# Queries of later groups loaded in 2-KB packets and put in order by four copies, and stores of two batches moved behind the loads

## The chip, the cores and the metric

The kernel runs on one core of one Trainium2 chip. The metric is device time in microseconds; the median of several executions is compared. One execution is also profiled, and its trace gives the instructions of each engine: TensorE (PE, with its weight loads as PEld), VectorE (DVE), ScalarE (ACT), GpSimd (POOL), and SyncE (SP), which here only issues DMAs.

## The reference

A decaying linear attention over 4 batches, 8 heads, 768 positions and 64 elements a head, followed by a mixture-of-depths feed-forward on its output, seen as 4 x 768 rows of 512.

```python
for b in range(nb):                       # blocks of 64 positions
    intra = einsum('bhic,bhjc->bhij', qb, kb) * Dmask[None]
    intra = einsum('bhij,bhjd->bhid', intra, vb)
    inter = einsum('bhid,bhde->bhie', qb * lam_pow[None], kv_state)
    out[:, :, sl] = intra + inter
    kv_state = lam_block * kv_state + einsum('bhsd,bhse->bhde', kb * rev_pow, vb)
...
scores = einsum('bsd,d->bs', x, w_gate)   # x: the attention's output, (4, 768, 512)
for b in range(B):
    top_idx = argpartition(-scores[b], capacity)[:capacity]   # capacity 128
    xe = x[b, top_idx]
    ye = maximum(xe @ w1, 0.0) @ w2       # 512 -> 1024 -> 512
    out[b, top_idx] = xe + sigmoid(scores[b, top_idx])[:, None] * ye
```

Everything is float32.

## The kernel before

**Groups.** The work is cut into 24 groups (NG) of 128 positions with all eight heads, six (NT) to a batch; group g belongs to batch g // 6. Groups 0 to 10 are "wide" (one state step for 128 positions), groups 11 to 23 work in two halves of 64 positions (WIDE = 11). The Python loop at L682 writes the order of every engine's instructions by hand (a manual schedule); nothing is reordered later, and each engine works through its own list and waits on semaphores.

**Loads.** `load(g)` (L66) issues three DMAs of 256 KB from SP: keys (kn), queries (qn), values (vn). Each tile has the 128 positions as partitions and the 8 x 64 elements of the heads behind each other, so that the DRAM side is 1024 runs of 64 floats (256 bytes). Eight sets of tiles exist (AHEAD), and `loads_to` (L656) decides how many groups ahead the loads stand in SP's list: 4 up to group 13, then one more for every two groups. The same function puts in the weights (w1 in four DMAs of 512 KB, w2 in eight of 256 KB, between groups 8 and 13). SP issues in order: a DMA that waits for its data holds all those behind it.

**One iteration g of the later groups** (L754 to L785), in PE's order: the queries and then the keys of group g+1 are transposed (L203, four 128x128 transposes each) into a PSUM bank each, from which ACT copies them to SBUF (L207); a first part of the feed-forward of an earlier batch (`products`; L564 for the first matrix, L576 for the second, or the transposes L535 of the gathered rows, copied by ACT at L540); group g's part from the states (L340); the state products of g+1 (L287); the column sums (L472) and the row transpose (L434) that rank the gate's scores; two more products, one before and one after the comparisons; group g's part from its masked scores (L363); and the scores of g+1 (L240). Then ACT copies the output from PSUM to `x_b` (L391 and two of 64 partitions at L393), SP stores it (L398), and VectorE forms the mask products and the gate's score.

GpSimd multiplies the queries by their powers (qs, L216), the states (decayed, L300) and the keys (kd, L185), and issues the indirect DMAs: the gather of a batch's 128 chosen rows from the output in DRAM (L522) and the scatter of their new values (L594, L603). The gather of batch b stands in iteration 6b + 9 (for the third batch, groups 12 to 17, in iteration 21) and needs all stores of that batch.

**PSUM.** Four banks go round (`bank`, L161): each transpose, product and row transpose takes the next one, and must wait until the copy out of it is done.

**Stores.** `store(g)` (L395) issues the stores that the table STORES lists for iteration g. Those of the second batch (groups 6 to 11) are kept back to iterations 11 to 13, every other group's store stands in its own iteration (those of 12 and 13 behind the kept ones).

Of the kernel before, what the change touches and what calls it, by code (L numbers as in the profile page):

```python
# [17 lines left out]
def kernel(  # L18
# [12 lines left out]
    nc = tc.nc  # L31
# [5 lines left out]
    L = 128  # L37
    C = 64
    NT = S // L
# [4 lines left out]
    NG = B * NT  # L44
# [4 lines left out]
    WEIGHTS = {8: 1, 9: 2, 10: 1, 11: 3, 12: 3, 13: 2}  # L49
    WIDE = 11  # L50
    WARM = 8
    TINY = 2.0 ** -125
    BELOW = TINY * (1.0 - 2.0 ** -24)

# [7 lines left out]

    half = [slice(0, C), slice(C, 2 * C)]
    loaded = {}

    def load(g):  # L66
        b, c = divmod(g, NT)
        rows = slice(c * L, (c + 1) * L)
        srcs = (("kn", k), ("qn", q), ("vn", v))
        tiles = [ld.tile([128, H, D], FP32, name=name) for name, _ in srcs]  # L70
        whole, front, back = slice(0, H), slice(0, H // 2), slice(H // 2, H)
        order = [(x, whole) for x in range(3)]
        if g == 0:
            order = [(0, front), (1, front), (0, back), (1, back), (2, whole)]
        for x, hs in order:
            if (g, x) == (2, 2):
                nc.sync.dma_start(
                    out=wg_b[:], in_=moe_w_gate.unsqueeze(0).broadcast_to([128, HD])
                )
            nc.sync.dma_start(  # L80
                out=tiles[x][:, hs], in_=srcs[x][1][b, hs, rows, :].rearrange("h p d -> p h d")
            )
        loaded[g] = tiles
# [3 lines left out]
    wg_b = const.tile([128, HD], FP32, name="wg_b")  # L87
    wg_o = const.tile([128, HD], FP32, name="wg_o")
    load(0)
    load(1)  # L90
    load(2)
    w1_sb = const.tile([128, NDC, F], FP32, name="w1_sb")
    w2_sb = const.tile([128, NFC, HD], FP32, name="w2_sb")
# [18 lines left out]
    for hp in range(NHP):  # L112
        for hh in range(2):
            h = 2 * hp + hh
            nc.vector.tensor_tensor_scan(
                out=mask_w[:, hh, hp, :], data0=lam_b[:, h : h + 1].broadcast_to([128, L]),
# [29 lines left out]
    o_ = psum.tile([128, 2, 512], FP32, name="o")  # L146
    free = [psum.tile([128, 512], FP32, name=f"m{i}") for i in range(4)]
    held = []
    KEPT = range(NT, 2 * NT)
    STORES = {11: [6, 7], 12: [8, 9, 12], 13: [10, 11, 13]}  # L150

    def warm(n):
        for _ in range(n):
            nc.tensor.matmul(
                free[-1][:, :L], lhsT=zero[:], rhs=zero[:], start=True, stop=True,
                skip_group_check=True,
            )

    warm(WARM)

    def bank(hold=False):  # L161
        t = next(t for t in free if not any(t is x for x in held))
        free[:] = [x for x in free if x is not t] + [t]
        if hold:
            held.append(t)
        return t

    qTs, qss, kTs, kds, ps_ = {}, {}, {}, {}, {}
# [23 lines left out]
    def transposes(g, name, part=None):  # L192
        if g >= NG:
            return
        t = loaded[g][1 if name == "qT" else 0]
        dsts = qTs if name == "qT" else kTs
        hps = range(NHP) if part is None else range(part * NHP // 2, (part + 1) * NHP // 2)
        if not part:
            banks_[name] = bank()
            dsts[g] = att.tile([128, NHP, L], FP32, name=name)  # L200
        tp = banks_[name]
        for hp in hps:
            nc.tensor.transpose(  # L203
                tp[:, hp * L : (hp + 1) * L], in_=t[:, 2 * hp : 2 * hp + 2, :], identity=ident[:]
            )
        at = slice(hps[0] * L, (hps[-1] + 1) * L)
        nc.scalar.copy(out=dsts[g][:].rearrange("p a i -> p (a i)")[:, at], in_=tp[:, at])  # L207

# [186 lines left out]
    def store(g):  # L395
        for n in STORES.get(g, [] if g in KEPT else [g]):
            b, t = divmod(n, NT)
            nc.sync.dma_start(  # L398
                out=out[b, t * L : (t + 1) * L, :],
                in_=x_bs[b][:, t].rearrange("p a b e -> p (a b e)"),  # L400
            )
# [222 lines left out]
    def constants():  # L624
        nc.gpsimd.memset(lead[:], TINY)
        nc.gpsimd.affine_select(
            out=lead[:], in_=lead[:], compare_op=ALU.is_ge, fill=-BELOW,
            base=0, pattern=[[1, L]], channel_multiplier=-1,
        )
        nc.gpsimd.memset(ones[:], 1.0)  # L630
        nc.gpsimd.iota(slot_i[:], pattern=[[1, 128]], base=0, channel_multiplier=0)
        nc.gpsimd.iota(place_i[:, 0], pattern=[[1, NG]], base=0, channel_multiplier=0)
        nc.gpsimd.iota(place_i[:, 1], pattern=[[0, NG]], base=0, channel_multiplier=1)
# [48 lines left out]
    for g in range(-1, NG):  # L682
# [3 lines left out]
        if wide(g):  # L686
# [7 lines left out]
            if g < 0:  # L694
                for part in range(2):
                    transposes(0, "kT", part)
                    transposes(0, "qT", part)
# [4 lines left out]
            elif g == 0:  # L702
                transposes(1, "kT")
                from_scores(0, 0)
                transposes(1, "qT")
                from_scores(0, 1)
                outputs(0)
                store(0)
                queries_decayed(1)
                nc.scalar.copy(  # L710
                    out=decay_w[:], in_=qpow[:, :, L - 1 : L].broadcast_to([128, NHP, D])
                )
                decay_state(2)
            else:
                for name in ("kT", "qT") if g == 1 else ("qT", "kT"):
                    transposes(g + 1, name)
                queries_decayed(g + 1)
                from_scores(g)
                if g == 1:
                    nc.scalar.copy(  # L720
                        out=wg_o[:].rearrange("p (a b e) -> p a b e", a=2, e=D),
                        in_=wg_b[:].rearrange("p (b a e) -> p a b e", a=2, e=D),
                    )
                    gate_scores(0)
                outputs(g)
                store(g)
                gate_scores(g)
# [113 lines left out]
```

## Time and profile before

| | |
|---|---|
| median of 3 runs | 178.64 us (177.48 to 182.0) |
| profiled execution | 179.35 us, span 177.6 us |
| PE busy | 161.5 us (91%), 3228 instructions |
| PEld busy | 133.7 us (75%) |
| VectorE busy | 99.1 us (56%) |
| GpSimd busy | 86.2 us (49%) |
| ScalarE busy | 68.9 us (39%), 173 instructions |
| SP's DMA queue | 81776 packets, 29.63 MB, 70.3% of 16 engines |
| chain that ended last | PE 61%, DMA 18%, SP's queue 8%, issue 4%, ACT 3% |

The span runs from the first to the last instruction of the program; the profiled execution's own time is 1.75 us longer. Busy shares are averages over the whole span: a chain is followed back from the last instruction to what released each step, so it names what the end waited for. Matmuls overlap in the array, so a busy PE is not a PE at its peak.

### The profile page before, as it was taken

To read this page: it belongs to the slowest core of one execution; us is meant where nothing else is said; L and a number is where in the kernel's file an instruction comes from. 1 tells how busy PE (TensorE), PEld (TensorE's weight loads), DVE (VectorE), ACT (ScalarE), POOL (GpSimd) and SP (SyncE) were. 2 spreads that over 40 slices of the span, in tenths; PEclk is the share of its full clock that TensorE was granted. 3 is DMA by queue.
4 is the path that set the end of the run, shared out by engine and by line. 5 is a ranking of instruction groups with operands and counts; after the bars stand their busy time and mean duration, and the time that the engine had idled before them with its cause. 6 is when DMAs were issued, how large, how long until landed. Compare 5 with 4: busy or idle time off the path is not lost.

```text
span 177.6 us, 7490 instructions
## 1 busy us (share of the span) xinstructions
PE 161.5 (91%) x3228; PEld 133.7 (75%) x3228; DVE 99.1 (56%) x304; ACT 68.9 (39%) x173; POOL 86.2 (49%) x96
## 2 busy tenths in 40 slices
PE   7998988999998999899695989999998999999990
PEld 7687966789887989897363679887665699559970
DVE  2876957678694748635627457647565767030011
ACT  3344436453343545434332364556244353013100
POOL 1396562546667656547374755827756300202022
PEclk9999999999999999999999999999999999999997
DMA  4999989999989999988989999999412131201000
GB/s 108 223 223 206 238 196 224 234 233 252 209 187 266 285 251 243 325 217 284 265 286 241 230 251 212 207 231 232 147 63 80 44 122 59 63 0 59 0 30 30
DMA packets 82608, 32.20 MB, mean 181 GB/s; under 512 B 75792, under 2 KB 77840, under 8 KB 82576
## 3 DMA queue, kind: packets, MB, share of 16 engines
q1 hardware_dynamic: 81776, 29.63, 70.3%
q0 software_dynamic: 656, 2.10, 3.9%
q8 instruction: 25, 0.41, 1.0%
q14 instruction: 7, 0.06, 0.1%
q10 hardware_dynamic: 144, 0.00, 0.0%
HBM read 24.38 MB, written 7.34 MB: 179 GB/s over the span
## 4 chain that ended last, share of the span: by engine, by line
PE 61%; DMA 18%; SPq 8%; issue 4%; ACT 3%; POOL 2%; DVE 2%; POOLq 1%; ACTq 0%
PE m L564 14%; PE m L576 11%; DMA qn<-in_q_dram 10%; PE m L203 9%; SPq L80 6%; PE o L356 4%; PE o L340 3%; DMA kn<-in_k_dram 3%; DMA wg_b<-in_moe_w_gate_dram 3%; PE o L363 3%; PE su L287 3%; PE su L240 3%; PE o L329 3%; PE su L234 2%; PE m L434 2%
## 5 line engine op out<-in xcount | busy, mean ns | idle before, releaser
L564 PE MATMUL m<-xsT,w_sb 128*128 128x128 f32 x256 | 31.3, 276 | 0.0
L564 PEld LDWEIGHTS m<-xsT,w_sb 128*128 128x128 f32 x256 | 30.0, 193 | 0.6 <-ACT xsT L540 0.6
L576 PE MATMUL m<-w_sb,hs 128*128 128x512 f32 (+1 forms) x80 | 30.1, 508 | 0.0
L216 POOL TENSOR_TENSOR qs<-qT,qpow 128x512 f32<-128x512 f32 x13 | 16.6, 1274 | 14.7 <-ACT qT L207 14.7
L300 POOL TENSOR_TENSOR decayed<-state,decay 128x256 f32<-128x256 f32 x21 | 16.5, 786 | 8.2 <-DVE ranks L476 6.2
L203 PE MATMUL m<-ident,qn 128*128 128x128 f32 x96 | 15.7, 283 | 5.1 <-DMA qn<-in_q_dram 4.6
L437 ACT COPY sc_row<-m 128x128 f32<-128x128 f32 x24 | 6.3, 266 | 32.6 <-PE m L434 23.5
L207 ACT COPY qT<-m 128x512 f32<-128x512 f32 (+1 forms) x25 | 14.2, 569 | 10.9 <-PE m L203 6.7
L576 PEld LDWEIGHTS m<-w_sb,hs 128*128 128x128 f32 x80 | 14.2, 193 | 5.6 <-issue 4.8
L185 POOL TENSOR_TENSOR kd<-kn,kpow 128x512 f32<-128x512 f32 x13 | 14.3, 1097 | 6.8 <-DMA kn<-in_k_dram 6.0
L185 POOL TENSOR_TENSOR kd<-kn,kpow_w 128x512 f32<-128x512 f32 x11 | 11.7, 1059 | 12.1 <-DMA kn<-in_k_dram 6.9
L207 ACT COPY kT<-m 128x512 f32<-128x512 f32 (+1 forms) x25 | 14.3, 574 | 6.0 <-PE m L203 6.0
L568 ACT ACTIVATE hs<-m 128x128 f32<-128x128 f32 x32 | 8.9, 279 | 17.9 <-PE m L564 17.9
L214 POOL TENSOR_TENSOR qs<-qT,qpow 128x512 f32<-128x512 f32 x9 | 11.5, 1274 | 8.8 <-ACT qT L207 8.6
L203 PEld LDWEIGHTS m<-ident,qn 128*128 128x128 f32 x96 | 10.3, 141 | 6.7 <-DMA qn<-in_q_dram 5.2
L203 PE MATMUL m<-ident,kn 128*128 128x128 f32 x96 | 14.8, 275 | 0.4 <-ACT kT L207 0.2
L319 DVE TENSOR_TENSOR state<-su,decayed 128x256 f32<-128x256 f32 x21 | 8.9, 424 | 9.9 <-POOL decayed L300 6.4
L254 DVE TENSOR_TENSOR p<-su,mask_w 128x1024 f32<-128x1024 f32 (+1 forms) x11 | 12.9, 1169 | 2.1 <-PE su L234 2.1
L356 PE MATMUL o<-vn,p 128*64 128x64 f32 x352 | 12.9, 225 | 0.2 <-DVE p L254 0.2
L356 PEld LDWEIGHTS o<-vn,p 128*64 128x64 f32 x352 | 11.3, 138 | 2.2 <-issue 1.4
L414 DVE CUSTOM_DVE_ANT_0 xg<-x_b,wg_b 128x512 f32<-128x512 f32 x14 | 11.4, 817 | 2.6 <-DMA wg_b<-in_moe_w_gate_dram 1.5
L407 DVE CUSTOM_DVE_ANT_0 xg<-o,wg_o 128x512 f32<-128x512 f32 x10 | 6.9, 690 | 10.2 <-ACT x_b L385 9.9
(86 smaller groups left out, 278.2 us busy)
## 6 DMA issues: line engine op xcount, KB each, us to landing
vn<-in_v_dram SPq DMA_DIRECT2D x24, 256.0 KB, 6.0
out_dram<-x_b SPq DMA_DIRECT2D x24, 256.0 KB, 4.7
kn<-in_k_dram SPq DMA_DIRECT2D x23, 256.0 KB, 5.1
qn<-in_q_dram SPq DMA_DIRECT2D x23, 256.0 KB, 5.1
w_sb<-in_moe_w_dram SPq DMA_DIRECT2D x4, 512.0 KB, 6.1
w_sb<-in_moe_w_dram SPq DMA_DIRECT2D x8, 256.0 KB, 4.8
kn<-in_k_dram SPq DMA_DIRECT2D x2, 128.0 KB, 3.3
qn<-in_q_dram SPq DMA_DIRECT2D x2, 128.0 KB, 3.4
```

What stands on the lines that cost most here:

```text
L80: nc.sync.dma_start(out=tiles[x][:, hs], in_=srcs[x][1][b, hs, rows, :].rearrange("h p d -> p h d"))
L185: nc.gpsimd.tensor_tensor(out=kd[:], in0=loaded[g][0][:], in1=pw[:].rearrange("p a b -> p (a b)").unsqueeze(2).broadcast_to([128, H, D]), ...
L203: nc.tensor.transpose(tp[:, hp * L : (hp + 1) * L], in_=t[:, 2 * hp : 2 * hp + 2, :], identity=ident[:])
L207: nc.scalar.copy(out=dsts[g][:].rearrange("p a i -> p (a i)")[:, at], in_=tp[:, at])
L214: nc.gpsimd.tensor_tensor(out=qs[:], in0=qTs[g][:], in1=qpow[:], op=ALU.mult)
L216: nc.gpsimd.tensor_tensor(out=qs[:].rearrange("p a (c i) -> p a c i", c=2), in0=qTs[g][:].rearrange("p a (c i) -> p a c i", c=2), in1=qpow ...
L254: nc.vector.tensor_tensor(out=ps_[g][:, :, at], in0=(o_ if part == 1 else su)[:, :, at], in1=mask_w[:].rearrange("p a b i -> p a (b i)")[: ...
L300: nc.gpsimd.tensor_tensor(out=t[:], in0=states[n][:], in1=(decay_w if wide(g) else decay)[:], op=ALU.mult)
L356: nc.tensor.matmul(o_[half[c], hh, hp * D : (hp + 1) * D], lhsT=p[:, hh, i0 : i0 + C], rhs=vn[:, 2 * hp + hh, :], start=(hp == 0 and g % N ...
L414: nc.vector.tensor_tensor_reduce(out=xg[:], in0=x_bs[b][:, t].rearrange("p a b e -> p (a b e)"), in1=wg_b[:], scale=1.0, scalar=0.0, op0=A ...
L564: nc.tensor.matmul(ph, lhsT=w1_sb[:, dc, f * 128 : (f + 1) * 128], rhs=keep["xsT"][:, dc, :], start=(dc == 0), stop=(dc == NDC - 1),)
L576: nc.tensor.matmul(py[:, e0:e1], lhsT=keep["hs"][:, f, :], rhs=w2_sb[:, f, e0:e1], start=(f == 0), stop=(f == NFC - 1),)
```

## The change

The queries of groups 12 to 23 are loaded in another layout. A partition is no longer a position but a head and a run of eight successive positions (RUN = 128 // 16): partition 16h + o holds positions 8o to 8o + 7 of head h, 512 floats that lie together in DRAM. The DMA has 128 runs of 2 KB in place of 1024 of 256 bytes. The four transposes of L203 now each take two of the eight positions of all runs, so that their columns come out by head and run and the rows by position parity and element. The copy from PSUM is therefore made of four, each of 64 partitions and 4 x 4 x 16 elements, two of which change the half of partitions; each writes elements that are eight floats apart. The tile qT that results is the same as before.

The stores of groups 12 to 23 leave their own iterations: those of the third batch are issued in pairs in iterations 18, 19 and 20, those of the fourth in pairs in iterations 21, 22 and 23. In SP's list the stores of groups 12 to 17 stood before loads 16 (12), 17 (13, behind 11), and between loads 18 and 23 (14 to 17, in their own iterations); now all twelve stand behind load 23. The number of stores and their size do not change.

```diff
+    RUN = L // 16
...
+    def packed(g):
+        return g > WIDE
...
         for x, hs in order:
...
+            if x == 1 and packed(g):
+                nc.sync.dma_start(
+                    out=tiles[1][:].rearrange("p t d -> p (t d)"),
+                    in_=q[b, :, rows, :].rearrange("h (o t) d -> h o (t d)", t=RUN),
+                )
+                continue
             nc.sync.dma_start(
                 out=tiles[x][:, hs], in_=srcs[x][1][b, hs, rows, :].rearrange("h p d -> p h d")
             )
...
-    KEPT = range(NT, 2 * NT)
-    STORES = {11: [6, 7], 12: [8, 9, 12], 13: [10, 11, 13]}
+    KEPT = range(NT, NG)
+    STORES = {
+        11: [6, 7], 12: [8, 9], 13: [10, 11], 18: [12, 13], 19: [14, 15], 20: [16, 17],
+        21: [18, 19], 22: [20, 21], 23: [22, 23],
+    }
...
+        if name == "qT" and packed(g):
+            to = qTs[g][:].rearrange("p b (o j r) -> p r b j o", j=RUN // 2, r=2)
+            fro = tp[:].rearrange("p (j b a o) -> p a b j o", j=RUN // 2, a=2, o=16)
+            for r, hh in ((0, 0), (1, 1), (1, 0), (0, 1)):
+                nc.scalar.copy(out=to[half[hh], r], in_=fro[half[r], hh])
+            return
         at = slice(hps[0] * L, (hps[-1] + 1) * L)
         nc.scalar.copy(out=dsts[g][:].rearrange("p a i -> p (a i)")[:, at], in_=tp[:, at])
```

## The prediction

> **What bounds the kernel now.** I read the page's slices first, then the chain that ended last, then the waits of TensorE (PE) in the stretch that the change touches, then the DMA queue's packets, and last ScalarE's (ACT) order of work in one iteration. Two strips of the page set the scene: PE and DMA by slices of 4.44 us.
>
> ```profile
> PE   7998988999998999899695989999998999999990
> ...
> DMA  4999989999989999988989999999412131201000
> ```
>
> The DMA engines are full from the second slice to slice 28 (about 122 us) and nearly idle after it. PE is nearly full from slice 22 (98 us) to the end; between, it dips to 6 and 5 (84 to 98 us). The chain of waits says what ended those dips:
>
> ```profile
> 83.78 5.21 DMA qn<-in_q_dram
> 89.03 0.67 PE m L203 x4
> ...
> 91.34 5.84 DMA qn<-in_q_dram
> 97.23 1.09 PE m L203 x8
> ...
> 166.14 4.05 PE m L576 x19
> ```
>
> PE stood at the transposes of L203 until the queries of groups 16 and 17 had landed, at 89.0 and 97.2 us. From 97.23 the chain is PE's own work down to 170 us. So a transfer that is made shorter before 97 us moves the end; one after it does not, unless it becomes late. The waits of PE between 52.9 us (first load of group 12) and 141 us show the prize:
>
> ```profile
> PE m L203 <- DMA qn<-in_q_dram: 4.0, 3, 1.9
> PE su L240 <- issue: 1.0, 2, 0.6
> ```
>
> 4.0 us in three waits (groups 15, 16, 17: 0.3, 1.9, 1.9) is all that quicker loads can give back. What remains between 97 and 141 us is waits marked issue, under 1 us a place.
>
> **The queries' loads.** Twelve loads (groups 12 to 23) go from 1024 packets of 256 B to 128 of 2 KB. What a packet costs comes from the DMA view of two stretches: 30 to 50 us, five groups' loads and three stores, and 128 to 150 us, four stores.
>
> ```profile
> DMA packets 15428, 4.65 MB, mean 232 GB/s; under 512 B 15038, under 2 KB 15038, under 8 KB 15422
> q1 hardware_dynamic: 15422, 4.56, 107.3%
> ```
> ```profile
> q1 hardware_dynamic: 576, 1.05, 12.9%
> ```
>
> The shares are of 16 engines. In the second stretch 12.9% of 16 x 22 us is 45.4 us for 4 x 128 packets of 2 KB: 89 ns each (the 64 others are tiny). In the first, 107.3% of 16 x 20 us is 343 us; less 384 x 89 ns it is 309 us for 15038 small packets: 20.6 ns each. An old load takes 64 x 20.6 = 1.32 us of each engine, a store 8 x 89 = 0.71 us. The new load takes 8 x 89 = 0.71 us if all 16 engines share it, as they share the stores and the w2 loads. But its source list is 8 heads x 16 runs, while every DMA of the trace has 128 rows outermost on both sides. If the split follows that outermost eight, eight engines carry 16 x 89 = 1.42 us each, and the others nothing; a 16-engine transfer behind it waits for those eight. No row decides. Bounds: -0.61 to +0.10 us per load; I take +0.10, since what sets the new load apart from the store's row is just the list that spreads it, and keep -0.61 for the range.
>
> The Trainium skill, DMA: Bandwidth & Descriptors, section Why a DMA increments its semaphore by 16 and not by 1, states that the number of engines is the largest up to 16 that divides the slowest dimension of both sides, which is eight here; its Rules for kernel authors warn of an outermost dimension under 16. By the page each load costs 1.42 us, by the store's row 0.71 us; no trace here shows such a load.
>
> **The stores.** In the SyncE (SP) queue the stores of groups 12 and 13 stand ahead of load 17 now, and that of 12 ahead of load 16 too; after, both stand behind load 23. That takes 0.71 us off the engines ahead of the queries of group 16 and 1.42 us ahead of those of 17. Stores 14 to 17 leave the queue between loads 18 and 23, where PE has left the DMA behind: worth nothing, covered by PE's own work.
>
> What waits behind the kept stores: only other stores, and the gather of the third batch (L522), which needs stores 12 to 17 and issues at 133.98 us. SP issues the last load at 121 us now; with four stores fewer in between (2.8 us) some 3 us sooner, then six stores at 0.71 us, and the last has landed 4.7 us (the page's median) after: near 127 us, 7 us of cover. If that cover went, GpSimd (POOL) would stand at the gather with the decayed states and keys behind it. Pairs at groups 22 and 23 change nothing: SP is idle there, so store 22 still goes when its copies end (141.7 us) and store 23 at 146.5 us, which the last gather waits for.
>
> So the queries of group 17 land 6 x 0.10 - 2 x 0.71 = **0.8 us sooner** (groups 12 to 16 0.1 to 0.4 us later or 0.2 sooner, taken up before 97 us). With the low bound it is 6 x 0.61 + 1.42 = 5.1 us, more than the stalls hold: 4.0 us.
>
> **The four copies.** One 128x512 copy (L207) becomes four of 64x256, written 32 bytes apart. The nearest row has that size, also with halves that change partitions: L393, 366 ns, two in 0.74 us. The qT copy holds ACT for 0.49 us up to the next one's start; four take 1.48 us: the queries are ready 0.9 us and the keys 1.0 us later, in twelve groups. No row shows the stride on a copy of this size. From above, L142 (8 elements a partition, strided, 206 ns) against L123 (4 elements, 193 ns) gives 3.25 ns an element and, with the 163 ns that the L207 and L393 rows leave as fixed part, 1.0 us a copy. I take 0.37.
>
> The Trainium skill, Advanced Engine Details and Errata, section SBUF Cachelines, speaks against the change: a step that leaves the 16-byte line at each access is penalised. It gives no figure; the L393 row, with runs of 256 bytes, cannot contradict it. By the row the copies take 1.5 us a group, by the rule more.
>
> Who waits? GpSimd's qs (L216) comes 0.9 us later, but the decayed state behind it already waits 0.9 us for VectorE's state (126.07 us: 0.92), so it is covered. PE needs the two PSUM banks back. ACT in iteration 18, before:
>
> ```profile
> 110.07 0.74 ACT L393 COPY x_b<-o 64x256 f32<-64x256 f32 x2
> 110.83 0.59 ACT L207 COPY qT<-m 128x512 f32<-128x512 f32 x1
> 111.32 0.59 ACT L207 COPY kT<-m 128x512 f32<-128x512 f32 x1
> 111.79 0.30 ACT L568 ACTIVATE hs<-m 128x128 f32<-128x128 f32 x1
> 112.49 0.27 ACT L437 COPY sc_row<-m 128x128 f32<-128x128 f32 x1 [0.40 <-PE m L434]
> ```
>
> The row transpose (L434, 112.15 us) reuses the queries' bank, now free at 112.3; the next product (L564, 112.3) the keys' bank, free at 110.83 + 1.48 + 0.59 = 112.9. PE loses **0.6 us** there. In iteration 17, xsT (L540) ends at 105.8 instead of 104.8 and its product starts at 106.05, or 105.5 without the 0.5 us issue wait before it: 0 to 0.3 us, taken 0.1. Iterations 19 to 22 have 0.6 us and more left. Iterations 11 to 16 pay in time that PE spends waiting for queries anyway.
>
> **Sum.** The profiled execution took 179.35 us, 177.6 of span and 1.75 around it; the median of the runs is 178.64, 0.7 under it. Span: 177.6 - 0.8 + 0.7 = 177.5, own time 179.25, at the median's level **178.5 us**: no change that can be told. About 2% (3.6 us) is what this kernel's measurement can tell from none.
>
> **Rivals.**
> *A. All 16 engines share the new load.* For it: the store and w2 rows, the only 2-KB rows. Against: the list of eight. The 4.0 us of query waits go, ACT's 0.7 stays: -3.3, 175.3 us at the median's level, just short of 2%; without the ACT cost 174.6. Chance 0.30, 0.22 of it past 2%.
> *B. Slow strided copies make ACT the bound.* At 0.7 us a copy (2.8 us a group) the queries' and keys' banks come back late from group 17 on: xsT at 107.2 for 106.05 (1.1); keys at 114.2 for 112.5 (1.7); at 120.25 for 119.4 (0.85); at 132.6 for 131.6 (1.0); queries at 139.3 for 138.7 (0.6). Together 5.3; with the 0.8 of the loads +4.5: 183.1 us. It decides from some 0.65 us a copy; at twice L393's time per element (0.57) it is 2.3 us. For it: no strided row. Against: L393. Chance 0.22.
> *C. Eight engines run slower than 89 ns a packet, or the kept stores reach the gather.* At 130 ns the load costs 2.1 us, +0.76 x 6 - 1.42 = +3.1, with ACT +3.8, and loads 18 to 23 push the stores 4.5 us towards the gather: 182.4 us. For it: the saturated queue. Against: half of the engines get less to do. Chance 0.08.
>
> **How the numbers follow.** Forecast 0.40, its own range 177 to 180.5 us. Faster: 0.22, from A. Slower: 0.20 of B and 0.06 of C. The rest, 0.52, is within 2%. The range reaches over A and to the start of B's price: 174.5 to 182.6 us.
>
> **What would show it.** Right: PE's wait for the queries of 16 and 17 is still there at 3 to 4 us in total, the DMA strip full but its share down, as eight engines idle in turns; L207's copies near 370 ns; L564 waiting for ACT kT in iteration 18. A is shown by PE without waits for qn after 60 us. B by L207 copies over 0.6 us and PE waiting for ACT in most iterations from 17. C by a landing time of qn above 6 us, or by POOL idle before L522 with a store as releaser. I am wrong outright if iterations before 60 us change, as nothing there is touched.

## The result, and the profile after

The changed kernel takes 183.52 us (median of 4 runs, 182.7 to 183.75) against 178.77 us beside it: 1.028 of the time before, with a 95% interval of 1.022 to 1.035. A second comparison, of six runs against 23 on one chip, gave 1.037 (1.030 to 1.043). Ratios here compare, where enough executions allow it, only those within 1.5% of the fastest of the same kernel, so they need not be the quotient of two medians. The profiled execution took 183.52 us, of which 181.7 are span (before 179.35 and 177.6).

Line numbers have moved: L216 is the transposes (L203 before), L223 the four new copies and L226 the plain one (both L207), L412 the output's copies (L393), L453 the row transpose (L434), L559 xsT (L540), L583 and L595 the products (L564, L576), L541 the gather (L522), L235 the powers of the queries (L216), L382 the part from the masked scores (L363), L587 the activation behind the first matrix (L568), L456 the copy of the row transpose (L437).

From the page of the kernel after: the busy times, three strips by slices of 4.54 us, the chain that ended last by engine and by line, and the group of the new copies (busy time, mean ns of one, idle time before them).

```profile
PE 164.1 (90%) x3228; PEld 134.8 (74%) x3228; DVE 97.2 (54%) x304; ACT 91.7 (50%) x209; POOL 85.3 (47%) x96
...
PE   7998999899899977999789969799989999999990
...
ACT  3344465444334649567385776695684754113100
...
DMA  5999999899999999989989999999210231101000
...
PE 44%; ACT 16%; issue 12%; DMA 8%; POOL 7%; SPq 6%; DVE 5%; POOLq 1%; ACTq 0%
PE m L583 13%; PE m L595 10%; ACT qT L223 10%; PE m L216 5%; SPq L90 5%; PE o L382 3%; DMA qn<-in_q_dram 3%; DMA vn<-in_v_dram 3%; PE o L375 3%; PE su L259 2%; POOL decayed L319 2%; ACT kT L226 2%; PE su L253 2%; ACT x_b L412 2%; PE o L348 1%
...
L223 ACT COPY qT<-m 64x256 f32<-64x256 f32 x48 | 29.8, 621 | 2.3 <-PE m L216 1.6
```

ACT's busy time has gone from 68.9 to 91.7 us, and ACT, with 3% of the chain before, holds 16% of it, 10% at L223 alone. The new copies take 621 ns each, not 370. The chain's share of issue (time in which an engine waited for nothing that the profile shows) has gone from 4 to 12%; no run explains that. The DMA strip looks as it did.

PE's waits over the whole span after (what waited, for what: total us, times, longest):

```profile
PE m L453 <- ACT qT L223: 3.1, 6, 0.7
PE m L583 <- ACT xsT L559: 1.6, 2, 0.8
PE m L583 <- ACT kT L226: 1.1, 4, 0.3
...
PE m L216 <- DMA qn<-in_q_dram: 0.4, 1, 0.4
```

The waits for queries, 4.6 us in four stretches before, are down to 0.4, and of the 4.0 us behind 52.9 us nothing is left. In their place PE waits 3.1 + 1.6 + 1.1 = 5.8 us in twelve stretches for banks and a tile that ACT copies late. Iteration 18 shows how, first ACT's timeline and then PE's (start, us; the bracket is the idle time before and what ended it):

```profile
111.65 0.74 ACT L412 COPY x_b<-o 64x256 f32<-64x256 f32 x2
112.42 2.52 ACT L223 COPY qT<-m 64x256 f32<-64x256 f32 x4
114.96 0.59 ACT L226 COPY kT<-m 128x512 f32<-128x512 f32 x1
115.44 0.28 ACT L587 ACTIVATE hs<-m 128x128 f32<-128x128 f32 x1
115.61 0.27 ACT L456 COPY sc_row<-m 128x128 f32<-128x128 f32 x1
```

```profile
114.99 0.32 PE L453 MATMUL m<-ident,sc 128*128 128x128 f32 x1 [0.73 <-ACT qT L223]
115.60 2.05 PE L583 MATMUL m<-xsT,w_sb 128*128 128x128 f32 x16 [0.29 <-ACT kT L226]
```

The queries' copies begin at 112.42 and the keys' copy at 114.96: 2.54 us, where before it was 0.49. The row transpose L453 needs the queries' bank and waits 0.73 us, the product behind it the keys' bank, another 0.29 us. The chain of waits runs through the same place:

```profile
112.42 0.62 ACT qT L223
113.05 0.63 ACT qT L223
113.70 0.61 ACT qT L223
114.32 0.62 ACT qT L223
114.96 0.60 ACT kT L226
115.60 2.05 PE m L583 x16
117.65 0.62 PE o L382 x32
```

Before, this stretch of the chain was PE's own work. The start of the queries' transposes marks the iterations; between two such starts, read off PE's timeline, each iteration took (us):

| iteration | 11 | 12 | 13 | 14 | 15 | 16 | 17 | 18 | 19 | 20 | 21 |
|---|---|---|---|---|---|---|---|---|---|---|---|
| before | 6.16 | 6.35 | 7.45 | 7.97 | 8.20 | 5.23 | 6.57 | 7.09 | 6.26 | 6.04 | 7.25 |
| after | 7.49 | 7.65 | 7.55 | 7.29 | 7.36 | 5.60 | 7.57 | 7.66 | 7.09 | 6.62 | 7.03 |

Iterations 11 and 12 lose 2.6 us; 14 and 15, which used to wait for queries, give back 1.5; 17 to 20, where before PE waited for no data (only 0.5 + 0.6 us marked issue), lose 28.94 - 25.96 = 3.0 us. Iteration 21 starts 4.0 us later than before (132.38 against 128.42), and the span is 4.1 us longer.

### The profile page after: what moved, and what is told of

The parts are those of the page before. It is cut to its first block, busy times and chain, and to the rows that moved or that the text cites. A ratio compares the mean times of both kernels' runs of the same rounds, so it can differ in the third digit from the quotient of the medians.

```text
span 181.7 us, 7530 instructions
## 1 busy us (share of the span) xinstructions
PE 164.1 (90%) x3228; PEld 134.8 (74%) x3228; DVE 97.2 (54%) x304; ACT 91.7 (50%) x209; POOL 85.3 (47%) x96
## 2 busy tenths in 40 slices
DMA packets 71760, 32.20 MB, mean 177 GB/s; under 512 B 63408, under 2 KB 65456, under 8 KB 71728
## 3 DMA queue, kind: packets, MB, share of 16 engines
q1 hardware_dynamic: 70928, 29.63, 70.3%
## 4 chain that ended last, share of the span: by engine, by line
PE 44%; ACT 16%; issue 12%; DMA 8%; POOL 7%; SPq 6%; DVE 5%; POOLq 1%; ACTq 0%
PE m L583 13%; PE m L595 10%; ACT qT L223 10%; PE m L216 5%; SPq L90 5%; PE o L382 3%; DMA qn<-in_q_dram 3%; DMA vn<-in_v_dram 3%; PE o L375 3%; PE su L259 2%; POOL decayed L319 2%; ACT kT L226 2%; PE su L253 2%; ACT x_b L412 2%; PE o L348 1%
## 5 line engine op out<-in xcount | busy, mean ns | idle before, releaser
L583 PE MATMUL m<-xsT,w_sb 128*128 128x128 f32 x256 | 31.9, 278 | 2.7 <-ACT xsT L559 1.6
L235 POOL TENSOR_TENSOR qs<-qT,qpow 128x512 f32<-128x512 f32 x13 | 16.5, 1268 | 37.8 <-ACT qT L223 37.2
L583 PEld LDWEIGHTS m<-xsT,w_sb 128*128 128x128 f32 x256 | 29.8, 192 | 4.5 <-ACT xsT L559 2.6
L223 ACT COPY qT<-m 64x256 f32<-64x256 f32 x48 | 29.8, 621 | 2.3 <-PE m L216 1.6
L595 PE MATMUL m<-w_sb,hs 128*128 128x512 f32 (+1 forms) x80 | 30.1, 508 | 0.0
L587 ACT ACTIVATE hs<-m 128x128 f32<-128x128 f32 x32 | 8.9, 278 | 19.5 <-PE m L583 19.5
L595 PEld LDWEIGHTS m<-w_sb,hs 128*128 128x128 f32 x80 | 14.3, 194 | 5.6 <-issue 4.8
L226 ACT COPY kT<-m 128x512 f32<-128x512 f32 (+1 forms) x25 | 14.3, 571 | 6.4 <-PE m L216 6.1
L216 PE MATMUL m<-ident,qn 128*128 128x128 f32 x96 | 16.1, 289 | 0.5 <-DMA qn<-in_q_dram 0.4
L456 ACT COPY sc_row<-m 128x128 f32<-128x128 f32 x24 | 6.4, 270 | 18.6 <-PE m L453 10.4
L216 PE MATMUL m<-ident,kn 128*128 128x128 f32 x96 | 15.3, 281 | 0.1
L273 DVE TENSOR_TENSOR p<-su,mask_w 128x1024 f32<-128x1024 f32 (+1 forms) x11 | 12.9, 1170 | 3.2 <-PE su L253 3.2
L198 POOL TENSOR_TENSOR kd<-kn,kpow 128x512 f32<-128x512 f32 x13 | 13.5, 1042 | 0.0
L375 PE MATMUL o<-vn,p 128*64 128x64 f32 x352 | 12.9, 225 | 0.2 <-DVE p L273 0.2
L382 PEld LDWEIGHTS o<-vn,p 64*64 64x64 f32 x416 | 7.6, 134 | 6.8 <-issue 3.7
L253 PE MATMUL su<-qT,kT 64*128 64x128 f32 x168 | 12.3, 285 | 0.1
```

The source lines that it names most:

```text
L198: nc.gpsimd.tensor_tensor(out=kd[:], in0=loaded[g][0][:], in1=pw[:].rearrange("p a b -> p (a b)").unsqueeze(2).broadcast_to([128, H, D]), ...
L216: nc.tensor.transpose(tp[:, hp * L : (hp + 1) * L], in_=t[:, 2 * hp : 2 * hp + 2, :], identity=ident[:])
L223: nc.scalar.copy(out=to[half[hh], r], in_=fro[half[r], hh])
L235: nc.gpsimd.tensor_tensor(out=qs[:].rearrange("p a (c i) -> p a c i", c=2), in0=qTs[g][:].rearrange("p a (c i) -> p a c i", c=2), in1=qpow ...
L253: nc.tensor.matmul(to[:, hh, hp * L : (hp + 1) * L], lhsT=kT[half[hh], hp, :], rhs=qT[half[hh], hp, :], start=True, stop=True, skip_group_ ...
L273: nc.vector.tensor_tensor(out=ps_[g][:, :, at], in0=(o_ if part == 1 else su)[:, :, at], in1=mask_w[:].rearrange("p a b i -> p a (b i)")[: ...
```

## The experiments

The theory after this result: the copies' writes, 32 bytes apart, are slow, and the late banks cost PE the time. Its rivals: the loads (eight engines), the stores' new places, or four copies in place of one, whatever their step. All ratios are against the kernel before on the same chip.

**1. The stores alone** (kernel before with the new KEPT and STORES).

```diff
-    KEPT = range(NT, 2 * NT)
-    STORES = {11: [6, 7], 12: [8, 9, 12], 13: [10, 11, 13]}
+    KEPT = range(NT, NG)
+    STORES = {11: [6, 7], 12: [8, 9], 13: [10, 11], 18: [12, 13], ... 23: [22, 23]}
```

> The kernel before with the new store table alone. Theory 1 (the strided copies cost the time, by banks given back late): 177.2 us, as two stores of 0.7 us leave the queue ahead of the queries of group 17. Theory 2 (the queries' loads, 12 percent of the bytes, on half of the engines cost it): the same, at most 178.5. Theory 3 (stores behind all loads press on the gather and the tail): 181 or more.

Measured: 0.998 (0.992 to 1.005), median 179.25 us against 179.57. PE's waits for queries remain (L206 is the transposes; the profiled execution, 181.5 us, is one of the longer ones):

```profile
PE m L206 <- DMA qn<-in_q_dram: 5.6, 3, 2.1
```

The stores' places are worth nothing that can be measured, either way; the 1.4 us that theory 1 expected of them did not show, though the interval just reaches it.

**2. The copies alone** (kernel before, plain loads and old stores).

```diff
+        if name == "qT" and g > WIDE:
+            to = qTs[g][:].rearrange("p b (o j r) -> p r b j o", j=4, r=2)
+            fro = tp[:].rearrange("p (j b a o) -> p a b j o", j=4, a=2, o=16)
+            for r, hh in ((0, 0), (1, 1), (1, 0), (0, 1)):
+                nc.scalar.copy(out=to[half[hh], r], in_=fro[half[r], hh])
+            return
```

> The kernel before, with the plain loads and old stores, and the four strided copies in place of the one for groups 12 to 23; the columns of the queries come out permuted, which changes no instruction's size. Theory 1: copies of 0.62 us, PE waits for ACT at L434 and L564, 181 to 183 us (a part hides in the query waits, which stay). Theory 2: under 179.5 us. Theory 3: 178.6.

Measured: 1.039 (1.020 to 1.057), copies of 622 ns. PE's waits (L440 is the row transpose, L570 the product of the first matrix, L546 xsT, L210 the four copies, L213 the plain one):

```profile
PE m L440 <- ACT qT L210: 3.1, 6, 0.8
...
PE m L203 <- DMA qn<-in_q_dram: 1.9, 4, 1.0
PE m L570 <- ACT xsT L546: 1.5, 2, 0.8
...
PE m L570 <- ACT kT L213: 1.1, 4, 0.3
```

The three waits for ACT are those of the changed kernel, within 0.1 us each, and iterations 17 to 20 take 28.91 us, against 28.94 there. The copies bring a loss of the whole size with the old loads and the old stores.

**3. Loads and stores with the one plain copy** (the changed kernel without the branch of L223).

> The changed kernel with the one plain 128x512 copy in place of the four; the queries stay in the order in which the packed load brings them. Theory 1: 174.5 to 176.5 us, PE waits for queries under 1 us. Theory 2: 181 us or more, with PE waiting for queries. Theory 3: 181 or more.

Measured: 1.022 (1.002 to 1.042), four runs from 176.6 to 183.5 us with a median of 180.95, so the 174.5 to 176.5 us of theory 1 did not come; the spread is too wide to use as a time. The profiled execution is the fastest of the four (176.62 us, span 174.8); it is of use for its waits (L220 is the plain copy):

```profile
PE m L216 <- DMA qn<-in_q_dram: 6.4, 6, 1.9
...
PE m L216 <- ACT kT L220: 0.7, 2, 0.5
```

The waits for xsT, for the queries' bank and for the keys' bank at the products are gone (0.7 us for the keys' copy are left, at the transposes), and iterations 17 to 20 take 25.1 us. But with exactly the loads of the changed kernel PE waits 6.4 us for queries, where theory 1 expected under 1. So the loads do not explain by themselves that the changed kernel had only 0.4 us left; that PE, held up by ACT, came later than the data is likely and not shown. These waits also differ between executions: in the profiled execution of the changed kernel under 4 they come to 3.0 us in three stretches, beside 1.9 + 1.6 + 1.1 us for ACT, and in that of the other order of loops to 0.4.

**4. The other order of loops** (the changed kernel; j innermost, so that ACT writes every second element, 8 bytes apart, four in a row, and reads 512 bytes apart).

```diff
-            to = qTs[g][:].rearrange("p b (o j r) -> p r b j o", j=RUN // 2, r=2)
-            fro = tp[:].rearrange("p (j b a o) -> p a b j o", j=RUN // 2, a=2, o=16)
+            to = qTs[g][:].rearrange("p b (o j r) -> p r b o j", j=RUN // 2, r=2)
+            fro = tp[:].rearrange("p (j b a o) -> p a b o j", j=RUN // 2, a=2, o=16)
```

> The changed kernel, same copies, but each walks the four pair indices j innermost, so that it writes at a step of 8 bytes (two elements to a 16-byte line, four to a run) and reads PSUM at a step of 512 bytes; the same data. Theory 1, if the step of 32 bytes on the written side is what slows a copy: 0.37 to 0.45 us a copy and 176 to 178.5 us. If the copy is slow for another reason (two PSUM halves, four dimensions, or the read side), 0.6 us or more and 183 us. Theories 2 and 3: 183.5.

Measured: 1.011 (1.000 to 1.022), copies of 388 ns. As this touched the interval of the changed kernel, both were run again, side by side on one chip:

> The changed kernel itself, beside e10, e11 and e12 on one chip, so that they can be compared with it directly. If the step of the copies' writes is the cause, it stands 3 to 5 us above e10 and some 2.8% above the kernel before. If the cause were the loads or the stores, e10 would be as slow as this.

> The changed kernel with the copies' loops in the other order (8-byte steps), as in e4. Copy theory: about 1.0 to 1.01 of the kernel before, 3 to 5 us under e9. Rival (loads or stores cost the time): within 1 us of e9.

Measured: the changed kernel 1.037 (1.030 to 1.043), the other order of loops 1.000 (0.995 to 1.005). The intervals lie far apart. The medians of all executions are 185.55 us (6), 181.57 (12) and, for the kernel before, 179.23 (23): by them the order of loops is worth 4.0 us, and 2.3 us of the loss would remain, which no run explains. One tile's line and ACT's timeline in iteration 18, of the second:

```profile
L223 ACT COPY qT<-m x48: 377/389/397, 62.2 to 140.2; 64x256 f32<-64x256 f32 x48
```

```profile
113.20 1.59 ACT L223 COPY qT<-m 64x256 f32<-64x256 f32 x4
114.82 0.59 ACT L226 COPY kT<-m 128x512 f32<-128x512 f32 x1
```

Four copies hold ACT for 1.62 us up to the keys' copy, against 2.54, and iterations 17 to 20 take 26.23 us, against 28.94 in both profiled executions of the changed kernel. The same data, the same number of copies and the same changes of partition: two rearranged axes make the difference.

**5. The copies alone, with 8-byte steps** (experiment 2 with the order of loops of 4).

> The kernel before with the four copies alone, written in 8-byte steps (the loads and stores are the old ones, and the queries' columns come out permuted). If only the 32-byte step costs time, copies near 388 ns, PE's waits for ACT under 2 us and the ratio within 1% of the kernel before, against 1.039 with 32-byte steps. If four copies in place of one cost as such (issue, semaphores, partition changes), the ratio stays above 1.02.

Measured: 1.006 (1.001 to 1.011), about 1 us. PE's waits:

```profile
PE m L203 <- DMA qn<-in_q_dram: 5.0, 4, 2.4
...
PE m L570 <- ACT xsT L546: 0.6, 1, 0.6
...
PE m L570 <- ACT kT L213: 0.2, 1, 0.2
```

So four copies as such cost about 1 us, and the 32-byte step the rest of the 1.039 of experiment 2 (which ran on another chip). Iterations 17 to 20 take 26.01 us, as in the kernel before.

**6. A step of 16 bytes** (the changed kernel; inside each pair of heads first j's lower bit, then the runs, and j's higher bit innermost).

```diff
+            to = qTs[g][:].rearrange("p b (o v w r) -> p r b w o v", v=2, w=2, r=2)
+            fro = tp[:].rearrange("p (v w b a o) -> p a b w o v", v=2, w=2, a=2, o=16)
```

> The changed kernel with the copies' loops ordered so that successive writes lie 16 bytes apart (j's lower bit outermost, then the runs, then its higher bit). If what costs is that each write leaves its 16-byte line, a copy takes as long as with 32 bytes, 622 ns, and the time is that of e9. If the line is 32 bytes or longer, a copy takes about 390 ns and the time is that of e10. A price that grows with the step would give some 460 ns.

Measured: 1.033 (1.023 to 1.042), and per copy:

```profile
L223 ACT COPY qT<-m x48: 597/622/642, 61.3 to 144.6; 64x256 f32<-64x256 f32 x48
```

For comparison the line of the changed kernel, with its 32 bytes:

```profile
L223 ACT COPY qT<-m x48: 608/622/633, 61.2 to 142.2; 64x256 f32<-64x256 f32 x48
```

Half the step, the same 622 ns, although reads are 1 KB apart here and 4 bytes there: the price does not grow with the step. Iterations 17 to 20 take 28.90 us, as in the changed kernel. The price appears between 8 and 16 bytes, where the second element of a 16-byte line is lost. Three steps were measured, and no run tells such a line from a limit on the step itself.

**7. The queries' load over 16 engines** (the run outermost and the head behind it, which changes the order of partitions; first with the one plain copy).

```diff
-                    in_=q[b, :, rows, :].rearrange("h (o t) d -> h o (t d)", t=RUN),
+                    in_=q[b, :, rows, :].rearrange("h (o t) d -> o h (t d)", t=RUN),
```

> The changed kernel with the source of the packed loads written with its 16 runs outermost and the heads inside, so that the partitions are run by run, and the one plain copy in place of the four; the queries stay in the order of the load. Against the one-copy run with the eight heads outermost it shows what the eight engines cost. If a load is spread by its outermost dimension: 8 tiny completion packets more for each of the 12 loads (71856 packets in all, not 71760), PE waits for queries of groups 13 to 17 under 2 us instead of 6.4, and 173 to 176 us. If the spread does not matter: the same waits and time as there.

> The 16-run load with the four copies that walk the pairs innermost (0.39 us a copy when read at the same step before), the data as the reference wants it. If both the step of the written side and the eight engines cost the changed kernel its time: 175 to 177.5 us. If only the copies did: 178 to 180 us, as with the eight heads outermost.

Measured: 1.001 (0.992 to 1.010) with one copy, 1.005 (0.997 to 1.013) with the four of 8-byte steps, which read PSUM here in the order of the new partitions. The medians, 180.22 and 181.02 us against 180.91 of the kernel before on that chip, lie above the 173 to 177.5 us expected if the eight engines were to cost much. The pages' packet counts, first of the changed kernel, then of this load with one copy:

```profile
DMA packets 71760, 32.20 MB, mean 177 GB/s; under 512 B 63408, under 2 KB 65456, under 8 KB 71728
```

```profile
DMA packets 71856, 32.20 MB, mean 181 GB/s; under 512 B 63504, under 2 KB 65552, under 8 KB 71824
```

The data are the same 128 packets a load, yet there are 96 more tiny ones, 8 for each of twelve loads. The four stores in the prediction's stretch left 16 tiny packets each; a load with the heads outermost therefore leaves 8, and runs on eight engines. PE's waits with the 16-engine load and one copy (L300 is the state products, L253 the scores):

```profile
PE su L300 <- issue: 3.0, 2, 2.0
PE su L253 <- issue: 1.6, 3, 0.9
...
PE m L216 <- issue: 1.1, 1, 1.1
PE m L216 <- DMA qn<-in_q_dram: 1.0, 2, 0.7
```

The waits for queries fall from 6.4 (experiment 3) to 1.0 us, but waits marked issue grow to 3.0 + 1.6 + 1.1 us (0.3 us in all in experiment 3), and the time stays at that of the kernel before. That is one profiled execution: with the four copies of 8-byte steps and the same load, PE still waits 2.9 us for queries.

**8. Two of the four copies on VectorE** (8-byte steps; 16 engines, then eight).

```diff
-                nc.scalar.copy(out=to[half[hh], r], in_=fro[half[r], hh])
+                if r == hh:
+                    nc.scalar.copy(out=to[half[hh], r], in_=fro[half[r], hh])
+                else:
+                    nc.vector.tensor_copy(to[half[hh], r], fro[half[r], hh])
```

> As the run before it in this call, but the two copies that change the half of partitions go to VectorE, so that ACT is busy with queries for 0.78 us instead of 1.56. If ACT's place in the order is what is left of the cost: 1 us less than that run, 174.5 to 176.5 us. If VectorE, whose copies stand behind the gate's score, brings the queries later: the same or 1 to 2 us more, PE waiting for VectorE at L434 or L564.

> The changed kernel (eight heads outermost) with pairs innermost and two of the copies on VectorE. If the spread over engines matters, 1 to 3 us more than the 16-run version of the same copies; if not, the same. Against the inner-run version with all copies on ACT it shows what ACT's extra 0.8 us a group costs: 0 to 1.5 us less.

Measured: 1.003 (0.995 to 1.011) and 1.012 (1.003 to 1.020). Copies of the first by engine:

```profile
L224 ACT COPY qT<-m x24: 384/391/412, 61.8 to 138.8; 64x256 f32<-64x256 f32 x24
L226 DVE COPY qT<-m x24: 418/424/428, 62.6 to 139.6; 64x256 f32<-64x256 f32 x24
```

VectorE takes longer for its half than ACT, and nothing is gained by the split. But these two runs are the only ones with the same split of the copies on one chip that differ in the engines of the load, and they differ: 179.8 to 181.13 us with 16 engines (median 180.69), 181.19 to 182.58 with eight (182.29). All four executions of one lie above all four of the other, by 1.6 us between the medians, as the expectation put it for the case that the spread matters. The copies take the same time in both (391 and 388 ns on ACT, 424 and 426 on VectorE). It is not the queries that PE waits for longer: in the profiled executions it waits 2.0 us for them with 16 engines and not at all with eight, so how eight engines would cost time is open, and the pair was run once. No version tried is measurably faster than the kernel before.

## Why the prediction was wrong

Forecast was no change, 178.5 us; the result lies above its range of 174.5 to 182.6 us. Rival B came, almost at its number: 183.1 us predicted at 0.7 us a copy, 183.5 measured at 0.62. Its signs came too: copies over 0.6 us, and PE waiting for ACT in iterations 17, 18 and 19, and before that in 11 to 13. That the number is so near is partly luck: between B's own two prices, 2.3 us at 0.57 us a copy and 5.3 at 0.7, a copy of 0.62 would cost some 3.5 us, or 181.3 us in all, and B had all of it from iteration 17 on, while 2.6 us were lost in 11 and 12. Point by point:

- **The four copies: the step that failed.** "No row shows the stride on a copy of this size. [...] I take 0.37." With the two bounds 0.37 and 1.0 us, I took the row nearest in shape (L393: same tile, same changes of partition), which writes runs of 256 bytes and so lacks the one thing that was new. Taking off the 163 ns that the prediction used as the fixed part, an element costs (622 - 163) / 256 = 1.79 ns against 0.79 in L393 and 0.88 at 8 bytes. So the copies of a group take 2.54 us where I had put 1.48, and the 0.7 us of ACT waits in the sum became 5.8. What I dismissed for want of a figure, the Trainium skill's Advanced Engine Details and Errata, section SBUF Cachelines (16-byte lines, at least two hits on a line needed), agrees with what experiments 4 and 6 show: two elements to a line 388 ns, one to a line 622, whether 16 or 32 bytes apart. The value should have been put between the bounds, and B, which began to decide at 0.65, made at least as likely as no change.
- **Where the banks would be missed: right in place, wrong in size.** L434 and L564 in iteration 18 and xsT in 17 were named; they cost 0.73 + 0.29 us in 18, and in 17 0.78 at xsT with another 0.62 at the row transpose. "Iterations 19 to 22 have 0.6 us and more left" held for 0.37 us copies, not for these.
- **"Iterations 11 to 16 pay in time that PE spends waiting for queries anyway": half right.** That is so of 13 to 15; 11, 12 and 16 had no such waits, and lost 2.6 and 0.4 us.
- **The loads: the split was right, its price is small.** Eight engines, by the tiny packets of experiment 7. Between the two bounds for the load lay 6 x 0.71 = 4.3 us ahead of the queries of group 17; on one chip 16 engines were 1.6 us quicker than eight (experiment 8). Across chips it is not separated: 1.005 (0.997 to 1.013) with 16 engines against 1.011 and 1.000 with eight.
- **The prices of the packets: not borne out.** "Its share down" did not come. The queue of SP, from the page after:

```profile
q1 hardware_dynamic: 70928, 29.63, 70.3%
```

  The share was 70.3% before too, so the packets took 1998 us of engine time before and 2044 after, where 20.6 and 89 ns a packet would have taken 12 x (1024 x 20.6 - 128 x 89) ns = 116 us off. With 16 engines (experiments 7 and 8) it is 2029 to 2080 us. The 89 ns come from a stretch with the queue at 12.9%; what a 2-KB packet of a load takes in the full queue no run isolates.
- **The stores: harmless, as said, but without the gain.** The 1.42 us that the sum credits to them did not show (experiment 1: 0.998, 0.992 to 1.005). The third batch's gather was not delayed; POOL after reaches it without idle time:

```profile
137.63 1.04 POOL L198 TENSOR_TENSOR kd<-kn,kpow 128x512 f32<-128x512 f32 x1
138.82 0.99 POOL L541 DMA_INDIRECT xs<-out_dram,tok  x1
```

- **The prize of 4.0 us was not there to be had at that size.** The profiled execution of experiment 7 with one copy has no wait for queries left behind 52 us and gains nothing, as PE's waits marked issue take their place. What those waits are is open: in these traces some begin or end near packets of the instruction queue, but with 25 packets in 181.7 us that can be chance, and it was not tested. Also open is experiment 3's own time.

## What to carry to other kernels

When a copy gets a new access pattern, price the pattern, not the tile: a row of the same size with contiguous writes says nothing about a strided one, and where only an unfavourable rule speaks, the value is not the favourable bound. Of the possible orders of loops of a strided copy take the one that puts two or more neighbouring elements of a 16-byte line behind each other; here this took the copy from 622 to 388 ns and the ratio from 1.037 to 1.000 (the median of all executions from 185.55 to 181.57 us) without any other change. A shorter wait for data is a gain only as far as the next release (here PSUM banks, then issue) lets PE start earlier, so look up that one before counting the prize.

## What the runs showed of the hardware that was not expected

- ScalarE's writes of float32 to SBUF in steps of 16 and of 32 bytes cost the same, 622 ns for 64x256; in steps of 8 bytes 388 ns, almost the 366 ns of a contiguous copy, although ACT then reads PSUM 512 bytes apart. VectorE took 424 to 426 ns for the same 8-byte pattern.
- A DMA's engines can be counted in the profile: the load with 8 outermost leaves 8 tiny packets, one with 16 outermost 16 (71760 against 71856 packets in all, over twelve loads).
- Halving the engines of twelve 256-KB loads in a saturated queue cost about 1.6 us of 181 in the one pair of runs that share a chip and the split of the copies (182.29 against 180.69 us, four executions each, ranges apart), without a longer wait of TensorE for these loads; the cause is open.
